# Cosformer attention into a GeGLU block: the third block of the feed-forward layer in groups with seven-product pairs, and the order of the blocks before it

## The chip, the cores and the metric

The kernel runs on one core of one Trainium2 chip. The metric is the device time of one execution, in microseconds. All times below are microseconds unless they are marked otherwise.

## The reference, cut to what matters

```python
# q, k, v: (8 batches, 8 heads, 576 positions, 64)
theta = np.pi / 2.0 * pos / S
phi(x) = concatenate([relu(x) * cos(theta), relu(x) * sin(theta)])   # 128 features
kv = einsum('bhsf,bhsd->bhfd', phi(k), v);  z = sum(phi(k), over s)
x  = (phi(q) @ kv) / (phi(q) @ z + 1e-6)         # as (4608 tokens, 512)
out = (gelu(x @ w_gate) * (x @ w_val)) @ w_out   # 512 -> 1536 -> 512
```

## The kernel before

**Tiling.** The 4608 tokens are nine blocks of 512 (block 0 to 8). A batch has 576 tokens, so that the batches lie across the blocks: block 3, tokens 1536 to 2047, takes the last 192 tokens of batch 2 and the first 320 of batch 3. Block n of the feed-forward layer is interleaved by hand with the attention of the next batch and with the output product of block n - 1. Nothing is scheduled by a planner: each engine, and the DMA queue of SP, executes what it was given in the order in which the program text issues it. A tile that has one buffer (`qT`, `vx`) is written again when the last reader of its old contents is done.

**Attention of a batch b.** The loads put q, k and v into staging buffers (`st`, which has three places, and for early batches `sm` and `fs`; `stage` says which). `prep` scales one ninth of q or k (128x256) with the cosine (VectorE, line 179) or the sine (ScalarE, line 177) into `phis`, which has three places, one for k; `prep_both` does q and k at once (128x512, lines 191 and 193). `cast_v` casts v into `vx`. `turn_q` turns the scaled q with two DMA transposes on SP into `qT`. `kv_unit` makes the 128x65 matrices of all heads with 72 small matmuls (line 270) in PSUM banks 6 and 7, and ScalarE copies them out. `nm_unit` makes the numerators and denominators of 128 tokens in two banks (6 and 7 if nothing else is said; line 311), and VectorE normalises them in three instructions (lines 322 to 324) into `x_sb`. `turn_x` turns that with DMA transposes on SP into `xT` of the block or blocks it belongs to (line 378); the first two batches are turned on TensorE instead (`turn_x_pe`, line 386, with a copy in line 390).

**A plain unit** (`gv_unit(n, jt)`, jt from 0 to 11) makes 128 of the 1536 hidden columns for 512 tokens: four matmuls of 512 columns against w_gate, a gelu on ScalarE (line 439), four against w_val (line 430), and the product on VectorE (line 442) into `hT`. Units take two pairs of banks in turn, (0, 1) and (2, 3). Where the tokens come late, the first units of a block are done in two halves of 256 tokens.

**A seven-product pair** (`Pair`) makes two hidden tiles for both matrices with seven products in place of eight, each four matmuls of 256 columns (line 650), from sums of the weights (S1 to S4 in `ws`, made by `w_sum`, line 616) and sums of the block's tokens (T1 to T4 in `fs`, made by `x_sum` on POOL, line 630). A **group** (`group`, line 700) is one pair and one plain unit with three slots of the other work between their products; four groups make a block. Blocks 4 and 5 are in groups, blocks 6 to 8 in pairs alone, blocks 0 to 3 in plain units.

**The output product** (`o_step`, `product`, line 547) is done from block 1 on in seven-product form too, 14 products of six matmuls of 256 columns for a block. The sums of hT that they need (`h_sum`, line 529) are made on VectorE for blocks 1 and 2 and on POOL from block 3 on. From block 3 on (`joint`) products 1 and 2 go into one bank one after the other, and one copy is saved.

**The order in blocks 1 to 3** stands in one loop (lines 985 to 1057) with tables: `COMING` and `q3` (what is scaled and cast in which step), `LOADS`, `SUMS`, and `t_kv`, `t_nm`, `t_turn` (the step of the kv matrices, of the first numerators and of the turn of q). In block 2 that is step 6 for kv of batch 3, steps 7 to 11 for its numerators, and the turn of its q comes after step 1. The last two tiles of batch 2 have their numerators in steps 0 and 1 of block 2.

Of the kernel before, what the change touches and what calls it, by code (L numbers as in the profile page):

```python
# [16 lines left out]
def kernel(  # L17
# [13 lines left out]
    nc = tc.nc  # L31
# [52 lines left out]
    def stage(name, b):  # L84
        early = {
            ("q", 1): 1, ("k", 1): sm, ("v", 1): fs, ("k", 2): 2, ("v", 2): 1,
            ("q", 3): fs, ("k", 3): 2, ("v", 3): 1,
            ("q", 5): 1, ("k", 5): 0, ("q", 7): 1, ("k", 7): 0,
        }
        at = early.get((name, b), "qkv".index(name))  # L90
        if isinstance(at, int):
            return st[:, at]
        return at[:, 0:NP * R * D].rearrange("p (m x) -> p m x", m=NP)
# [71 lines left out]
    def phi_tile(name, b):  # L165
        phi[name, b] = phis[:, 1 if name == "k" else 2 * (b % 2) * (b > 3)]
        return phi[name, b]
# [370 lines left out]
    def product(n, p, i, u, m, v):  # L538
# [5 lines left out]
        last = n == NB - 1  # L544
        joint = not last and n > 2
        for j in range(JH):
# [15 lines left out]
        if i in (6, 7) or i == (2 if joint else 1) or last and i == 5:  # L562
            k, of = (1, u) if i == 2 else (i, at)
            got[key, k] = place(n, p, f"u{k}", CH, FP32)
            (dve_copy if n in (3, 4) else act_copy)(got[key, k], of)  # L565
        if i == (2 if last or joint else 1):
# [268 lines left out]
    q1 = {9: (0, 1, 2), 10: (3, 4, 5), 11: (6, 7, 8)}  # L835
    early_sums = {5: ("S1", 0), 6: ("S1", 512), 7: ("S3", 0), 8: ("S3", 512)}
    for jt in range(4, JT):
        gv_unit(0, jt)
        if jt in early_sums:
            name, j0 = early_sums[jt]  # L840
            w_sum(name, j0, j0 + 512)
        if jt == 5:
            turn_j(0, 0, 4, (R - 1,), 4, act_copy)
        if jt == 6:
            nm_unit(0, 4)
        if jt == 8:
            turn_x_pe(0, 4, 5, act_copy)
        if jt in q1:
            prep("q", 1, 0, q1[jt])
            prep("q", 1, 1, q1[jt], eng=nc.scalar)  # L850
# [46 lines left out]
    def js(a, b):  # L897
        return tuple(range(a, b))

    COMING = {  # L900
        2: {
            3: [("k", 3, js(0, 3))], 4: [("k", 3, js(3, 6)), ("v", 3, 0)],
            5: [("k", 3, js(6, 9)), ("v", 3, 2)],
            7: [("q", 4, js(0, 3))], 8: [("q", 4, js(3, 6))], 9: [("q", 4, js(6, 9))],
            10: [("k", 4, js(0, 3))], 11: [("k", 4, js(3, 6))],
        },
        3: {
            0: [("k", 4, js(6, 9))], 1: [("v", 4, 0)], 2: [("v", 4, 2)],
            7: [("qk", 5, js(0, 2))], 8: [("v", 5, 0), ("qk", 5, js(2, 4))],
            9: [("v", 5, 2), ("qk", 5, js(4, 6))], 10: [("qk", 5, js(6, 8))],  # L910
            11: [("qk", 5, js(8, 9))],
        },
    }
    casts = {
        (3, 0): act_copy, (3, 2): act_copy, (4, 0): act_copy, (4, 2): dve_copy,
        (5, 0): nc.gpsimd.tensor_copy, (5, 2): nc.gpsimd.tensor_copy,
    }
    LOADS = {
        (1, 11): [(3, "k"), (3, "v")],
        (2, 1): [(4, "q", 0, 4), (4, "q", 4, R)], (2, 6): [(4, "k"), (4, "v")],  # L920
        (2, 10): [(5, "k")], (3, 0): [(5, "q")], (3, 2): [(5, "v")],
        (3, 10): [(6, "q", 0, 5), (6, "k", 0, 5)],
        (4, 0): [(6, "q", 5, R), (6, "k", 5, R), (6, "v")],
# [4 lines left out]
        2: {0: "1", 1: "2", 2: "34", 3: "56", 6: "78"},  # L928
        3: {0: "1", 1: "23", 2: "4", 3: "56", 4: "7", 6: "8"},
        8: {i: str(i + 1) for i in range(8)},  # L930
    }
    for n in range(4, 8):
        SUMS[n] = {0: "1", 1: "23", 2: "4", 3: "5", 4: "6", 5: "7", 6: "8"}


    MORE = {}
    for n in (4, 5, 6):
        for i in range(4):
            MORE.setdefault((n - 1, 8 + i), []).append((n, i))
# [6 lines left out]
    def more(n, jt):  # L946
# [6 lines left out]

    q3 = {
        (1, 8): ((0,), (0, 1)),
        (1, 9): ((1,), (2, 3)),
        (1, 10): ((2,), (4, 5)),
        (1, 11): ((3, 4, 5), (6, 7)),
        (2, 0): ((6, 7), (8,)),
        (2, 1): ((8,), ()),  # L960
    }

    def late_of(b):
        return -(-(BLK - 64 * b) // 128)

    def o_step(n, jt):
        p, u = divmod(jt, 6)
        for i in ((1, 2) if n > 3 else (2, 1), (5,), (6,), (7,), (4,), (3,))[u]:
            product(n - 1, p, i, ps[:, 4, 0:CH], ps[:, 5, 0:CH], ps[:, 4, CH:C])
        for i in map(int, SUMS[n].get(jt, "")):  # L970
            eng = nc.gpsimd if n > 3 else nc.vector
            h_sum(n - 1, i // 5, f"S{(i - 1) % 4 + 1}", eng=eng)
# [10 lines left out]

    turn[0] = 1
    for n in range(1, 4):
        b = n + 1

        t_kv, t_nm, t_turn = {1: (7, 9, 12), 2: (6, 7, 11), 3: (3, 5, 9)}[n]
        for jt in range(JT):
            if n == 1 and jt >= t_nm:  # L990
                nm_unit(2, jt - t_nm, (6, 4, 6)[jt - t_nm])
                turn_x(2, jt - t_nm)
            heads = (0, 2, 4, 4)[n]
            if jt >= heads:
                gv_unit(n, jt, to=(2, 6) if (n, jt) == (3, JT - 1) else None)
            else:
                for i in range(2):
                    half, unit = divmod(2 * jt + i, heads)
                    gv_unit(n, unit, half * HALF, HALF)
                    if n == 1:  # L1000
                        j = JA + 2 * jt + i
                        prep("q", b, 1, (j,), eng=nc.scalar)
                        prep("q", b, 0, (j,))
                        if jt == i == 0:
                            turn_x_pe(1, 3, 5, dve_copy)
            i = jt - t_nm - 1
            if n > 1 and 0 <= i < late_of(b):
                turn_x(b, i)
            if n > 1:
                o_step(n, jt)  # L1010
            elif jt % 3 == 1:
                flush()
            if n == 1 and jt == 2:
                prep("q", b, 0, (R - 1,))
                prep("q", b, 1, (R - 1,), eng=nc.scalar)
                turn_q(b)
                nm_unit(1, NT - 1)
            if n == 1 and jt == 3:
                turn_x(1, NT - 1)
            nms = [(b, jt - t_nm)] if n > 1 and 0 <= jt - t_nm < NT else []  # L1020
            if n == 2 and jt < 2:
                nms.append((n, 3 + jt))
            for bt in nms:
                nm_unit(*bt)
            if jt == t_kv:
                kv_unit(b)
            if n == 1 and jt in (2, 3, 4):
                prep_third("k", b, jt - 2)
            if n == 1 and jt == 5:
                cast_v(b, 0, 4, dve_copy)  # L1030
            if (n, jt) in q3:
                cosines, sines_ = q3[n, jt]
                prep("q", 3, 1, sines_, eng=nc.scalar)
                prep("q", 3, 0, cosines)
            for name, c, what in COMING.get(n, {}).get(jt, ()):
                if name == "v":
                    cast_v(c, what, what + 2, casts[c, what])
                elif name == "qk":
                    for j in what:
                        prep_both(c, 0, j, nc.scalar if j % 2 else nc.vector)  # L1040
                        prep_both(c, 1, j, nc.scalar)
                else:
                    prep(name, c, 0, what)
                    prep(name, c, 1, what, eng=nc.scalar)
            c = {(2, 1): 2}.get((n, jt), b if n > 1 and jt == t_turn else None)
            if c is not None and n < 3:
                turn_q(c + 1)
            start_loads(n, jt)
            c = {(2, 1): 2, (3, 2): 3, (3, 9): 4}.get((n, jt))
            if c is not None:  # L1050
                for i in range(late_of(c), NT):
                    turn_x(c, i)
            if n == 3 and 3 <= jt < 7:
                w_sum(("S2", "S2", "S4", "S4")[jt - 3], (1 - jt % 2) * 512, (2 - jt % 2) * 512)
            if n == 1 and 4 <= jt < 8:
                wo_sum(("T3", "T1", "T2", "T4")[jt - 4])
            more(n, jt)

# [6 lines left out]
    def preps(n, jt):  # L1067
        b = n + 1
        if 4 <= b < B - 1:
            for what in PREPS.get(jt, "").split():  # L1070
                prep_both(b + 1, "cs".index(what[0]), int(what[1]), nc.scalar)

    def numerators(n, jt):
        b, t = n + 1, {6: 0, 7: 1, 9: 2, 10: 3, 0: 4}.get(jt)
        if jt == 0:
            b = n
        if t is not None and b > 4:
            nm_unit(b, t)
# [27 lines left out]
    def slot(n, jt):  # L1106
        if (n, jt) != (4, 0):
            o_step(*divmod(n * JT + jt - 1, JT))
# [11 lines left out]
    old, made = None, 0  # L1120
    for n in range(4, NB):
        groups = {4: 4, 5: 4}.get(n, 0)
        for g in range(groups):
# [61 lines left out]
```

## Time and profile before

| | |
|---|---|
| three runs | 310.57, 310.44, 310.0 (median 310.44) |
| the profiled execution | 311.0 |
| its span, first to last instruction | 309.0 |
| granted TensorE clock | 1.0 |
| TensorE busy | 296.7 |
| VectorE, ScalarE, POOL busy | 234.4, 193.9, 137.6 |

PE is TensorE's matmuls, PEld its weight loads, DVE VectorE, ACT ScalarE, POOL GpSimd and SPq the DMA queue of SyncE. A line of the timeline or of the groups gives start and length, the engine, the line of the kernel, the operation and its tiles as out<-in; in square brackets stands the idle time of the engine before it and what ended it. A line of the waits gives who waited for whom, the sum, the number of times and the longest. In the chain, each line is a piece of the path that ended last: start, length, what.

### The profile page before, as it was taken

To read this page: it belongs to the slowest core of one execution; us is meant where nothing else is said; L and a number is where in the kernel's file an instruction comes from. 1 tells how busy PE (TensorE), PEld (TensorE's weight loads), DVE (VectorE), ACT (ScalarE), POOL (GpSimd) and SP (SyncE) were. 2 spreads that over 40 slices of the span, in tenths; PEclk is the share of its full clock that TensorE was granted. 3 is DMA by queue.
4 is the path that set the end of the run, shared out by engine and by line. 5 is a ranking of instruction groups with operands and counts; after the bars stand their busy time and mean duration, and the time that the engine had idled before them with its cause. 6 is when DMAs were issued, how large, how long until landed. Compare 5 with 4: busy or idle time off the path is not lost.

```text
span 309.0 us, 7855 instructions
## 1 busy us (share of the span) xinstructions
PE 296.7 (96%) x3032; PEld 223.6 (72%) x3055; DVE 234.4 (76%) x513; ACT 193.9 (63%) x393; POOL 137.6 (45%) x118
## 2 busy tenths in 40 slices
PE   8899999999999989999999999999999999999993
PEld 3574466645876668665778787878898988888882
DVE  5855896799896897789678967894678785766782
ACT  7864774866468756349597858785546456465530
POOL 6775440000000000017854686579965866297410
PEclk9999999999999999999999999999999999999999
DMA  7999999974698999993999799937732421203035
GB/s 273 257 185 245 313 308 398 302 116 70 187 230 155 281 325 229 280 195 78 261 118 352 177 176 140 357 69 114 120 76 53 80 44 36 54 16 68 2 80 127
DMA packets 71637, 53.66 MB, mean 174 GB/s; under 512 B 45392, under 2 KB 59472, under 8 KB 71600
## 3 DMA queue, kind: packets, MB, share of 16 engines
q1 hardware_dynamic: 61824, 41.17, 59.1%
q0 software_dynamic: 9696, 11.93, 16.8%
q8 instruction: 24, 0.39, 0.5%
q14 instruction: 13, 0.11, 0.2%
q10 hardware_dynamic: 80, 0.07, 0.1%
HBM read 37.75 MB, written 9.44 MB: 153 GB/s over the span
## 4 chain that ended last, share of the span: by engine, by line
PE 75%; DMA 9%; issue 5%; ACT 4%; DVE 3%; POOL 1%; SPq 1%; POOLq 0%; ACTq 0%; DVEq 0%
PE ps L650 24%; PE ps L430 23%; PE ps L547 18%; PE ps L463 3%; PE ps L311 3%; DMA st<-in_v_dram 3%; DMA qT<-phis 2%; DMA xT<-x_sb 2%; ACT phis L191 2%; PE ps L270 2%; DMA st<-in_k_dram 2%; ACT phis L177 1%; ACT gel L439 1%; PE ps L233 1%; PE ps L401 1%
## 5 line engine op out<-in xcount | busy, mean ns | idle before, releaser
L430 PE MATMUL ps<-xT,wv_sb 128*128 128x512 bf16 (+1 forms) x253 | 56.8, 345 | 0.4 <-ACT gel L439 0.3
L430 PE MATMUL ps<-xT,wg_sb 128*128 128x512 bf16 (+1 forms) x240 | 54.5, 344 | 2.8 <-DMA xT<-x_sb 1.2
L442 DVE TENSOR_TENSOR hT<-gel,ps 128x512 bf16<-128x512 f32 (+1 forms) x64 | 38.2, 602 | 15.5 <-PE ps L430 13.6
L439 ACT ACTIVATE gel<-ps 128x512 f32<-128x512 f32 (+1 forms) x64 | 33.7, 528 | 24.6 <-PE ps L430 22.3
L208 POOL CAST vx<-st 128x1152 bf16<-128x1152 f32 x6 | 7.1, 1179 | 91.8 <-DMA st<-in_v_dram 91.8
L430 PEld LDWEIGHTS <-wv_sb 128*128 128x128 bf16 x256 | 25.0, 98 | 20.5 <-issue 0.4
L529 POOL TENSOR_TENSOR sm<-hT 128x768 bf16<-128x768 bf16 x20 | 32.8, 1638 | 15.8 <-PE ps L650 11.5
L547 PEld LDWEIGHTS <-sm 128*128 128x128 bf16 x336 | 32.9, 98 | 6.8
L430 PEld LDWEIGHTS <-wg_sb 128*128 128x128 bf16 x256 | 23.3, 98 | 16.7 <-DMA xT<-x_sb 1.4
L650 PE MATMUL ps<-fs,ws 128*128 128x256 bf16 x240 | 34.5, 273 | 0.2 <-ACT ps L669 0.2
L650 PEld LDWEIGHTS <-ws 128*128 128x128 bf16 x320 | 30.2, 98 | 4.1 <-ACT ps L669 0.5
L682 ACT ACTIVATE gel<-ps 128x512 f32<-128x512 f32 x26 | 15.5, 597 | 28.0 <-PE ps L650 28.0
L177 ACT ACTIVATE phis<-st,sin_t 128x256 bf16<-128x256 f32 (+1 forms) x75 | 31.5, 484 | 2.2 <-DMA st<-in_k_dram 1.3
L560 DVE TENSOR_TENSOR o_sb<-sm,ps 128x256 f32<-128x256 f32 x56 | 23.5, 419 | 12.1 <-ACT sm L565 11.0
L547 PEld LDWEIGHTS <-hT 128*128 128x128 bf16 x288 | 28.2, 98 | 5.4
L690 DVE TENSOR_TENSOR ps<-fs,ps 128x512 f32<-128x512 f32 x26 | 18.1, 696 | 18.0 <-PE ps L650 13.7
L650 PE MATMUL ps<-xT,wg_sb 128*128 128x256 bf16 x208 | 31.2, 273 | 0.0
L324 DVE TENSOR_TENSOR x_sb<-ps,rec 128x512 bf16<-128x512 f32 x38 | 26.3, 692 | 1.3
L547 PE MATMUL ps<-wo_sb,hT 128*128 128x256 bf16 x192 | 23.7, 273 | 0.0
L547 PE MATMUL ps<-T,sm 128*128 128x256 bf16 x168 | 22.9, 273 | 0.1
L650 PEld LDWEIGHTS <-wg_sb 128*128 128x128 bf16 x208 | 20.1, 98 | 4.0
L547 PE MATMUL ps<-wo_sb,sm 128*128 128x256 bf16 x168 | 22.9, 273 | 0.0
(126 smaller groups left out, 563.1 us busy)
## 6 DMA issues: line engine op xcount, KB each, us to landing
out_dram<-o_sb SPq DMA_DIRECT2D x69, 128.0 KB, 2.5
st<-in_v_dram SPq DMA_DIRECT2D x12, 576.0 KB, 6.9
st<-in_k_dram SPq DMA_DIRECT2D x8, 576.0 KB, 5.1
st<-in_q_dram SPq DMA_DIRECT2D x4, 640.0 KB, 5.9
st<-in_q_dram POOLq DMA_DIRECT2D x4, 576.0 KB, 12.4
st<-in_q_dram SPq DMA_DIRECT2D x4, 512.0 KB, 5.1
wg_sb<-in_moe_w_gate_dram POOLq DMA_DIRECT2D x6, 256.0 KB, 6.4
wv_sb<-in_moe_w_val_dram POOLq DMA_DIRECT2D x6, 256.0 KB, 7.3
```

Of the source, the lines that this page charges most:

```text
L177: nc.scalar.activation(o, i, AF.Relu, scale=tab[:, j:j + 1])
L311: nc.tensor.matmul(bank(b0 + h // 4)[:, (h % 4) * (D + 1):(h % 4 + 1) * (D + 1)], lhsT=q_cols(b, t, h), rhs=kv_sb[b][:, h // 2, h % 2, :], ...
L324: nc.vector.tensor_tensor(x, nm[:, :, :, 0:D], rec[:, :, :, None].to_broadcast([128, 2, 4, D]), op=ALU.mult,)
L430: nc.tensor.matmul(bank(to[g])[:, 0:w], lhsT=wt[:, ct, js], rhs=xt[:, ct, c0:c0 + w], start=(ct == 0), stop=(ct == CT - 1),)
L439: nc.scalar.activation(gel[:, 0:w], bank(to[0])[:, 0:w], AF.Gelu)
L442: nc.vector.tensor_mul(hT[n][:, jt, c0:c0 + w], gel[:, 0:w], bank(to[1])[:, 0:w])
L529: eng.tensor_tensor(a[name][:, j0:j1], a[x][:, j0:j1], a[y][:, j0:j1], op=op)
L547: nc.tensor.matmul(at, lhsT=hs.setdefault(key, h_parts(n, p))[a][:, j], rhs=ts[b][:, j], start=(j == 0 and i in ((1, 2, 4, 5), (1, 4, 5))[ ...
L560: nc.vector.tensor_tensor(o, got[key, k], x, op=op)
L650: nc.tensor.matmul(to[:, 256 * half:256 * half + 256], lhsT=w_part(a, j * 128, (j + 1) * 128)[:, ct], rhs=xb[self.n][b][:, ct], start=(hal ...
L682: nc.scalar.activation(self.gel0, self.other, AF.Gelu)
L690: nc.vector.tensor_tensor(bank(val), self.m5, self.sum, op=ALU.add)
```

## The change

Block 3 joins blocks 4 and 5 in groups, so that its tokens' sums, its hidden sums' place on POOL and the joint products 1 and 2 begin one block earlier. All eight halves of the weights' sums are made in block 0. The loop over blocks 1 to 3 becomes one function for block 1 and one for block 2:

- Batch 2: v is cast on ScalarE in steps 3 and 4 of block 1 (before: on VectorE in step 5); the kv matrices come in step 6 (before: 7); the first numerators come inside unit 9, between its two matmul groups (before: ahead of it). The turn of batch 1's fourth tile goes between the two matmul groups of block 1's first unit.
- Batch 3: k is loaded in step 2 and v in step 5 of block 1 (before: both at the end of its step 11), k into `sm`; q is scaled in steps 5 to 9 of block 1 into a place of its own, k in steps 10 and 11; q is turned after step 11. In block 2 v is cast in step 0, the kv matrices come in step 1, the numerators in steps 5 to 9, and each turn of x one step after its numerators, ahead of the loads of that step.
- Batch 4: q and k are loaded from step 10 of block 1 on and scaled together in steps 2 to 10 of block 2, v is cast on POOL. Batch 5 is loaded from step 9 of block 2 on and scaled in block 3, as batch 6 is in block 4.

```diff
@@ def stage
-            ("q", 3): fs, ("k", 3): 2, ("v", 3): 1,
+            ("q", 3): fs, ("k", 3): sm, ("v", 3): 2,
@@ def phi_tile
-        phi[name, b] = phis[:, 1 if name == "k" else 2 * (b % 2) * (b > 3)]
+        phi[name, b] = phis[:, 1 if name == "k" else 2 * (b % 2) * (b > 2)]
@@ def product
-        joint = not last and n > 2
+        joint = not last and n > 1
-            (dve_copy if n in (3, 4) else act_copy)(got[key, k], of)
+            (dve_copy if n in (2, 3, 4) else act_copy)(got[key, k], of)
@@ block 0
-    early_sums = {5: ("S1", 0), 6: ("S1", 512), 7: ("S3", 0), 8: ("S3", 512)}
+    early_sums = {4: ("S1", "S3"), 5: ("S2", "S4"), 6: ("S1",), 7: ("S3", "S2"), 8: ("S4",)}
@@ LOADS
-        (1, 11): [(3, "k"), (3, "v")],
-        (2, 1): [(4, "q", 0, 4), (4, "q", 4, R)], (2, 6): [(4, "k"), (4, "v")],
-        (2, 10): [(5, "k")], (3, 0): [(5, "q")], (3, 2): [(5, "v")],
-        (3, 10): [(6, "q", 0, 5), (6, "k", 0, 5)],
+        (1, 2): [(3, "k")], (1, 5): [(3, "v")],
+        (1, 10): [(4, "q", 0, 5), (4, "k", 0, 5)], (1, 11): [(4, "q", 5, R), (4, "k", 5, R)],
+        (2, 1): [(4, "v")],
+        (2, 9): [(5, "q", 0, 5), (5, "k", 0, 5)],
+        (3, 0): [(5, "q", 5, R), (5, "k", 5, R), (5, "v")],
+        (3, 9): [(6, "q", 0, 5), (6, "k", 0, 5)],
@@ def o_step
-            eng = nc.gpsimd if n > 3 else nc.vector
+            eng = nc.gpsimd if n > 2 else nc.vector
@@ the loop over blocks 1 to 3, now two functions
+    def scale(b, name, sines_, cosines):
+        for j in sines_:
+            prep(name, b, 1, (j,), eng=nc.scalar)
+        for j in cosines:
+            prep(name, b, 0, (j,))
+
+    SCALE = {
+        2: (2, "k", js(0, 3), js(0, 3)), 3: (2, "k", js(3, 6), js(3, 6)),
+        4: (2, "k", js(6, 9), js(6, 9)),
+        5: (3, "q", js(0, 1), ()), 6: (3, "q", js(1, 3), js(0, 1)),
+        7: (3, "q", js(3, 5), js(1, 3)), 8: (3, "q", js(5, 7), js(3, 6)),
+        9: (3, "q", js(7, 9), js(6, 9)),
+        10: (3, "k", js(0, 4), js(0, 4)), 11: (3, "k", js(4, 9), js(4, 9)),
+    }
+
+    def block1():
+        b, n = 2, 1
+        for jt in range(JT):
+            i = jt - 9
+            if i > 0:
+                nm_unit(b, i, (6, 4, 6)[i])
+                turn_x(b, i)
...
+                    x3 = lambda: turn_x_pe(1, 3, 5, dve_copy)
+                    gv_unit(n, unit, half * HALF, HALF, between=x3 if jt == i == 0 else None)
...
+                gv_unit(n, jt, between=(lambda: nm_unit(b, 0, 6)) if i == 0 else None)
...
+            if jt == 6:
                 kv_unit(b)
+            if jt in SCALE:
+                c, name, sines_, cosines = SCALE[jt]
+                scale(c, name, sines_, cosines)
+            if jt in (3, 4):
+                cast_v(b, 2 * (jt - 3), 2 * (jt - 3) + 2, act_copy)
+            if jt == 11:
+                turn_q(3)
             start_loads(n, jt)
...
+    EARLY = {
+        2: "s0", 3: "c0 s1 c1", 4: "s2 c2", 5: "s3 c3", 6: "s4 c4", 7: "s5 c5", 8: "s6 c6",
+        9: "s7 c7", 10: "s8 c8",
+    }
+
+    def block2():
+        b, n = 3, 2
+        for jt in range(JT):
...
+            if 0 <= jt - 6 < NT:
+                turn_x(b, jt - 6)
+            o_step(n, jt)
+            if 0 <= jt - 5 < NT:
+                nm_unit(b, jt - 5)
+            if jt < 2:
+                nm_unit(2, 3 + jt)
+            if jt == 0:
+                cast_v(b, 0, 2, dve_copy)
+                cast_v(b, 2, 4, act_copy)
+            if jt == 1:
+                kv_unit(b)
+            for what in EARLY.get(jt, "").split():
+                part = "cs".index(what[0])
+                prep_both(4, part, int(what[1]), nc.scalar if part or jt > 7 else nc.vector)
+            if jt == 1:
+                turn_x(2, 3)
+                turn_x(2, 4)
+            start_loads(n, jt)
+            if jt in (7, 8):
+                m = 2 * (jt - 7)
+                cast_v(4, m, m + 2, nc.gpsimd.tensor_copy)
             more(n, jt)
@@ the blocks in groups
-    for n in range(4, NB):
-        groups = {4: 4, 5: 4}.get(n, 0)
+    for n in range(3, NB):
+        groups = 4 if n < 6 else 0
```

`SUMS`, `MORE` (the sums of the tokens), `preps`, `numerators` and `slot` take block 3 in where they began with block 4.

## The prediction

> **What bounds the kernel now.** I read the page first, for busy shares.
>
> ```profile
> span 309.0 us, 7855 instructions
> PE 296.7 (96%) x3032; PEld 223.6 (72%) x3055; DVE 234.4 (76%) x513; ACT 193.9 (63%) x393; POOL 137.6 (45%) x118
> ```
>
> TensorE is the bound, at a granted clock of 1.0 throughout, so time is won by giving it fewer columns or fewer waits. Then busy time by stretch, cut where the blocks 1 to 5 begin on TensorE:
>
> ```profile
> core 0: us, PE busy (x) PEld busy (x) DVE busy (x) ACT busy (x) POOL busy (x), PEclk, DMA share, GB/s
> 54.20:78.40 24.20, 23.39 (x221) 13.27 (x222) 21.63 (x54) 16.95 (x40) 0.00 (x0) 1.00 0.70 155
> 78.40:113.30 34.90, 33.45 (x340) 23.80 (x340) 29.29 (x82) 23.21 (x54) 0.00 (x0) 1.00 1.00 241
> 113.30:146.60 33.30, 32.71 (x321) 23.07 (x325) 27.86 (x61) 19.61 (x41) 7.11 (x6) 1.00 0.90 201
> 146.60:178.10 31.50, 30.80 (x332) 24.36 (x334) 24.83 (x48) 23.57 (x41) 19.89 (x14) 1.00 0.96 227
> 178.10:209.30 31.20, 30.99 (x340) 24.95 (x343) 24.30 (x50) 23.15 (x41) 21.72 (x15) 1.00 0.91 181
> ```
>
> The first figure is the length, the next TensorE's busy time. Blocks 4 and 5 are already grouped and take 31.5 and 31.2; block 3 has the same attention and output products and takes 33.3. In block 1 VectorE is busy 21.63 of 24.20: the fullest engine after TensorE, and the change gives it more there. TensorE's waits between 54 and 160 us, and the chain around two of them:
>
> ```profile
> PE ps L430 <- DMA xT<-x_sb: 1.2, 1, 1.2
> PE ps L430 <- DVE xT L390: 0.5, 1, 0.5
> ```
>
> ```profile
> 65.47 7.25 DMA qT<-phis
> ...
> 106.39 6.91 DMA xT<-x_sb
> 113.35 1.92 PE ps L430 x16
> ```
>
> The transpose of 106.39 lands after 6.91 us, where the issue itself is 1.2: four loads were issued from 101.86 to 104.68 and it lands behind them. TensorE stood from 111.92 to 113.35. Last, the timeline, for the two things that I expect to decide:
>
> ```profile
> 101.14 0.42 PE L311 MATMUL ps<-kv_sb,qT 128*128 128x65 bf16 x8
> ...
> 102.03 0.69 DVE L324 TENSOR_TENSOR x_sb<-ps,rec 128x512 bf16<-128x512 f32 x1
> ...
> 102.64 0.87 DVE L179 TENSOR_SCALAR phis<-st,cos_t 128x256 bf16<-128x256 f32 x3
> ```
>
> ```profile
> 133.05 0.42 PE L311 MATMUL ps<-kv_sb,qT 128*128 128x65 bf16 x8
> ...
> 135.35 0.69 DVE L324 TENSOR_TENSOR x_sb<-ps,rec 128x512 bf16<-128x512 f32 x1
> ...
> 136.10 0.42 PE L311 MATMUL ps<-kv_sb,qT 128*128 128x65 bf16 x8 [0.25 <-DVE x_sb L324]
> ```
>
> From the first: VectorE normalises the numerators of banks 6 and 7 by 102.72, 1.25 after TensorE is through with them (101.47), and a 0.69 instruction holds VectorE for 0.61 before the next starts. From the second: whoever writes banks 6 and 7 next waits until that has ended (136.04, then 136.10).
>
> **What the change wins.** Block 3 in groups: each of four pairs runs 28 matmuls of 256 columns for what was 32, at 0.109 each (eight start in 0.87), 4 x 4 x 0.109 = 1.74 of TensorE. Its products, numerators, scalings, value casts and x sums become those of block 4 one batch earlier, so I take block 4's length for it: 33.3 to 31.5, 1.8. The sums for the products go from VectorE (0.55 each) to POOL (1.64) as in block 4, where POOL is busy 19.89 of 31.5. Block 4 is then no longer the first in groups and takes block 5's length, 0.3. The wait at 113.35 goes, 1.4 with its issue gap: numerators of batch 3 come at steps 5 to 9 of block 2 instead of 7 to 11, and their transposes stand on SP behind no load issued in those steps before step 9. I put the last that block 3 needs at about 110, the block at about 115, which leaves POOL 4 x 1.15 for the x sums. At the start of block 1 the turn of the last x moves between the two matmul groups of the first unit; the second half starts at 56.3 instead of 56.98, 0.7. The wait for qT at 72.45 (0.3 lost) goes, since the numerators come half a unit later. In all 4.5.
>
> **What it costs.** W sums: four more in block 0, at 0.61 of VectorE each. Adding the queue up from unit 4 (eight sums, five products of 0.60, one numerator set of 1.04), VectorE is up to 0.4 late and free again at 35.3, before the product due at 35.68. So 0; if that cover is gone, the turn of q waits for its cosines at 39, up to 0.4. Nothing there leaves TensorE's path, so it cannot gain.
>
> Value casts of batch 2 go from VectorE (1.36) to ScalarE (2 x 1.15, in units 3 and 4). ScalarE falls 2.4 behind by the gelu of unit 5; the bank it frees is wanted only after kv of batch 2, which now stands between units 6 and 7 with 1.27 of work. So 0; without that cover 0.7.
>
> Scaling of k of batch 3 moves into units 10 and 11 of block 1, behind which VectorE still has the numerators' normalising and products. Its queue from the product of unit 2 (at 59.9 with the 0.7 won) to the normalised x of batch 2's last tile in block 2: ten products x 0.60, 28 cosines x 0.26, four sets of numerators x 1.04, four sums of w_out x 0.87, together 21.0; then four half products x 0.33, two sets x 1.04, a cast 0.67, two sums x 0.46, one addition 0.33, together 5.3; and 1.5 in which it waits for ScalarE's late gelus and one copy. That ends at 87.7. The same sum for the old order ends the product of unit 11 at 79.8, against 79.66 in the trace, so I take 87.5.
>
> Two waits follow. At the start of block 2 the second unit reuses the bank pair of unit 11, whose product ends at about 80.8; and x of batch 2 lands behind the loads of k and v of batch 3, now issued in block 1 after qT (landed at 72.0 then, four loads at 1.5 each, 78.7). TensorE, which came 1.0 early, finishes unit two 0.5 later than before: cost 1.5, between 0 (no backlog) and 2.5 (first load 2.7 behind qT, as at 98.57 to 101.22 now).
>
> The second: kv of batch 3 moves from step 6 of block 2 to step 1, directly behind the numerators of batch 2's last tile, both in banks 6 and 7. Queued behind that wait on TensorE is everything. TensorE arrives at 85.2 (84.64 now plus 0.5), VectorE frees the banks at 87.5: 2.3. The floor with an idle VectorE is 1.25, from the row above. It can't be zero, since the banks are the same. The Trainium skill's page "PSUM — Partial Sum Buffer", in its summary of rules for kernel authors, wants a matmul to go to another bank than the one being read; no run yet shows this change with other banks, but by that rule kept the sum would be 2.3 lower.
>
> On SP, turning q of batch 3 waits for those same numerators (qT has one buffer), and the second halves of q and k of batch 4, two turns of x and v of batch 4 queue behind it. It landed 10.9 after issue at 61.84 and 13.0 in block 4; numerators of batch 3 come 13.2 after (kv 1.4, four steps of 2.4, the hold). I take 0, up to 0.5.
>
> **The sum.** 311.0 profiled (309.0 and 2.0 around the span) - 4.5 + 1.5 + 2.3 = 310.3. The profiled run lies 0.56 over the median of 310.44, so on the median 309.7.
>
> **Rivals.** (A) VectorE keeps up: for it, each engine's row sums are averages with 2.6 idle in block 1; against it, the work added there. Then nothing at block 2's start and 1.25 for the banks: -3.2, 307.2. (B) VectorE's queue is longer than added up: den, rec and x start with gaps of 0.03 between them; if all 68 instructions of the queue paid that, 2.0 more before kv, so +1.3, 311.7: slower. It decides from 88.8 on for the normalised x (the forecast has 87.5). For it, that the whole stretch is one queue with no slack; against it, that rows of 0.69 do start 0.60 apart. (C) The loads in block 1 land x of batch 2 at 80.1: block 2 begins 1.4 later, but VectorE catches up meanwhile, the hold shrinks to 1.3 or so, net about -0.3, 310.1. (D) The loads of batch 4 hold x of batch 3 after all, and the wait before block 3 stays: 1.4 more, 311.1; the transposes' place argues against it.
>
> **How the numbers follow.** Forecast 0.36 (own range 308.9 to 310.5), A 0.22, B 0.22, C 0.12, D 0.08. What the measurement can tell from no change is 0.2%, 0.62: below 309.82 faster, above 311.06 slower. Faster: A and 0.25 of the forecast, 0.47. Slower: B, D in part, together 0.30. The rest, 0.23, is C, D and the forecast's upper end. The range of 308.0 to 311.8 leaves out the far end of A and of B.
>
> **What would show it.** Right: block 3 about 31.5 long; no wait on xT before it; in block 2 a wait of kv (L270) on x_sb (L324) of 1.3 to 2.5; VectorE without idle from about 68 to 87. Wrong: no such wait (A), or one over 3.5 (B), or a wait on xT before block 2 of over 2 (C) or before block 3 (D), or a grouped block 3 longer than 32.

## The result, and the profile after

| | before | after |
|---|---|---|
| median of four runs each, on the same chip | 310.5 (310.0 to 311.74) | 320.66 (318.71 to 321.46) |
| ratio | | 1.0312, interval 1.0256 to 1.0368 |
| profiled execution, its span | 311.0, 309.0 | 321.46, 319.7 |
| mean granted clock in it | 1.000 | 0.977 |

The change makes the kernel slower by 3.1%. The forecast was 309.7, with a range of 308.0 to 311.8. Executions over 1.5% above the shortest of their kernel (two in run 1 below, one in 6, three in 9, one in 11) are left out of the ratios, while the medians are of all. From the page of the kernel after, busy time of TensorE and its granted clock in 40 slices:

```profile
PE   7799999999579979999999999999999999999992
PEclk9799999999789979999999999999999999999999
```

The losses lie in slices 11 to 15, 80 to 120 us. The row of the clock, all nines before, has four dents: one in the start (slice 2) and one in each of the slices 11, 12 and 15, where PE has its dents. Busy time by stretch, cut where the first matmuls of block 0, 1, 3, 4 and 5 stand, and for block 2 where its first could have stood (length first, then TensorE):

```profile
core 0: us, PE busy (x) PEld busy (x) DVE busy (x) ACT busy (x) POOL busy (x), PEclk, DMA share, GB/s
18.15:56.20 38.05, 37.50 (x375) 22.35 (x377) 28.60 (x68) 23.17 (x49) 15.40 (x22) 1.00 1.21 295
56.20:79.60 23.40, 23.24 (x221) 13.28 (x221) 21.21 (x56) 20.83 (x48) 0.00 (x0) 1.00 0.98 225
79.60:125.53 45.93, 37.73 (x337) 26.06 (x340) 30.69 (x73) 21.25 (x44) 6.84 (x6) 0.89 0.77 172
125.53:156.50 30.97, 30.53 (x329) 24.25 (x331) 22.88 (x47) 22.97 (x40) 19.72 (x14) 1.00 0.85 200
156.50:187.47 30.97, 30.76 (x338) 24.72 (x341) 24.08 (x50) 23.06 (x40) 19.83 (x14) 1.00 0.94 207
```

Against the same stretches of before (38.02, 24.20, 34.90, 33.30, 31.50): block 0 has the same length, block 1 is 0.8 shorter, block 3 2.3 and block 4 0.5, and block 2 grew from 34.9 to 45.9. That is 7.4 more. Nearly all of the rest of the 10.7 between the spans is at the two ends: block 0 starts 2.0 later (18.15 against 16.18), and from the last matmul to the end it takes 6.2 against 5.05. The late start is not the change's: over the profiles of this study it is 16.2 to 18.2 whatever the kernel, and 18.08 in one that differs from the kernel before only in block 1 and later. It goes with the dent in slice 2: in the six profiles in which the clock falls at about 11 us block 0 begins at 17.0 to 18.2, in the ten others at 16.2 to 17.1. TensorE's waits:

```profile
PE ps L430 <- DMA xT<-x_sb: 3.5, 1, 3.5
PE ps L270 <- DVE x_sb L324: 2.3, 1, 2.3
PE ps L311 <- DVE x_sb L324: 2.2, 1, 2.2
```

So there are three holes in block 2 (stretches in which TensorE waits), and a clock that drops after each.

**The first hole: x of batch 2 is late.** SyncE's queue, and the piece of the chain that ends the wait:

```profile
71.72 1.87 SPq L98 DMA_DIRECT2D sm<-in_k_dram  x2
73.68 1.17 SPq L378 DMA_TRANSPOSE xT<-x_sb  x1
75.03 0.96 SPq L98 DMA_DIRECT2D st<-in_v_dram  x2
76.93 3.61 SPq L378 DMA_TRANSPOSE xT<-x_sb  x2
```

```profile
76.93 6.29 DMA xT<-x_sb
83.21 0.14 issue
83.35 3.35 PE ps L430 x16
```

The transpose of 76.93 is issued in time and lands 6.29 later, behind k, x of batch 1 and v. In the kernel before the transposes of this stretch landed 2.4 to 3.1 after their issue. TensorE stood from 79.8 to 83.35.

**The second hole: kv of batch 3 waits for the banks.** The chain just ahead of it:

```profile
90.30 0.75 DVE vx L208
91.05 0.66 DVE hT L442 x2
91.71 0.47 DVE sm L529
92.29 0.21 DVE rec L323
92.52 0.70 DVE x_sb L324
93.27 2.16 PE ps L270 x72
```

A cast, two half products and a sum stand on VectorE ahead of the normalising that frees banks 6 and 7. VectorE brings no lateness there from block 1: behind the first hole it has nothing to do for 1.40.

```profile
85.32 0.42 DVE L442 TENSOR_TENSOR hT<-gel,ps 128x256 bf16<-128x256 f32 x1 [1.40 <-PE ps L430]
```

**The third hole, which the forecast did not have.** The timeline before the numerators of step 7:

```profile
109.69 1.14 POOL L208 CAST vx<-st 128x1152 bf16<-128x1152 f32 x1 [64.30 <-DMA st<-in_v_dram]
109.75 1.48 DVE L529 TENSOR_TENSOR sm<-hT 128x768 bf16<-128x768 bf16 x1
111.12 1.15 POOL L208 CAST vx<-st 128x1152 bf16<-128x1152 f32 x1 [0.29 <-PE ps L430]
111.17 1.51 DVE L529 TENSOR_TENSOR sm<-hT,sm 128x768 bf16<-128x768 bf16 x1
113.77 0.60 PE L311 MATMUL ps<-kv_sb,qT 128*128 128x65 bf16 x8 [2.15 <-DVE x_sb L324]
```

Two of VectorE's sums, 0.55 each elsewhere, take 1.48 and 1.51. Each begins 0.05 to 0.06 behind a cast of v of batch 4 on GpSimd and ends 0.40 to 0.41 behind that cast's end. The Trainium skill's page "SBUF — State Buffer", section "SBUF: two separate sides", says that GpSimd and a VectorE instruction with two SBUF inputs take a shared pair of ports as an exclusive lock for a whole instruction. The rows nearly agree: a sum that waits for the whole cast would end 0.55 behind it, and these ended 0.40 and 0.41 behind.

**The clock.** Stretches of 3.41 us, cut at the instants at which the granted clock changes; PEclk, the granted clock, is the third figure from the end:

```profile
79.50:82.92 3.42, 0.30 (x2) 0.00 (x0) 3.35 (x11) 2.79 (x7) 0.00 (x0) 1.00 1.34 226
82.92:86.34 3.42, 2.99 (x15) 2.10 (x16) 1.42 (x5) 0.62 (x2) 0.00 (x0) 0.50 1.09 348
86.34:89.75 3.41, 3.41 (x39) 3.08 (x38) 1.65 (x6) 1.85 (x5) 0.00 (x0) 1.00 0.30 82
89.75:93.17 3.42, 1.18 (x17) 1.06 (x15) 3.35 (x8) 0.28 (x2) 0.00 (x0) 1.00 0.28 42
93.17:96.58 3.41, 3.31 (x78) 2.89 (x78) 0.04 (x1) 0.74 (x3) 0.00 (x0) 0.50 0.90 130
110.23:113.64 3.41, 1.38 (x10) 0.80 (x9) 3.34 (x6) 1.11 (x2) 1.75 (x2) 1.00 0.26 17
113.64:117.06 3.42, 3.29 (x15) 1.42 (x15) 2.43 (x7) 0.60 (x1) 0.00 (x0) 0.50 0.44 90
```

All changes lie on one grid of 3.41. A stretch in which TensorE was busy 0.30, 1.18 or 1.38 is followed by one at half clock, that is at a granted clock of 0.50. So each hole costs its length and then up to half of 3.41 again.

### The profile page after: what moved, and what is told of

It reads as the page before. It is cut to its first block, busy times and chain, and to the rows that moved or that the text cites. A ratio compares the mean times of both kernels' runs of the same rounds, so it can differ in the third digit from the quotient of the medians.

```text
span 319.7 us, 7881 instructions
## 1 busy us (share of the span) xinstructions
PE 299.6 (94%) x3047; PEld 228.4 (71%) x3071; DVE 231.8 (73%) x497; ACT 198.9 (62%) x390; POOL 155.6 (49%) x132
## 3 DMA queue, kind: packets, MB, share of 16 engines
q0 software_dynamic: 9696, 11.93, 16.2%
## 4 chain that ended last, share of the span: by engine, by line
PE 80%; DVE 5%; issue 5%; DMA 4%; ACT 2%; POOL 1%; SPq 0%; POOLq 0%; DVEq 0%; ACTq 0%
PE ps L650 28%; PE ps L430 20%; PE ps L547 19%; PE ps L463 3%; PE ps L311 3%; PE ps L270 3%; DMA st<-in_v_dram 2%; DMA xT<-x_sb 2%; PE ps L233 1%; DVE sm L529 1%; ACT phis L177 1%; DVE hT L442 1%; PE ps L401 1%; DVE x_sb L324 1%; PE ps L386 1%
## 5 line engine op out<-in xcount | busy, mean ns | idle before, releaser
L430 PE MATMUL ps<-xT,wg_sb 128*128 128x512 bf16 (+1 forms) x190 | 47.4, 366 | 4.5 <-DMA xT<-x_sb 3.5
L529 POOL TENSOR_TENSOR sm<-hT 128x768 bf16<-128x768 bf16 x24 | 39.4, 1643 | 20.8 <-DVE hT L442 9.8
L430 PE MATMUL ps<-xT,wv_sb 128*128 128x512 bf16 (+1 forms) x206 | 49.5, 363 | 0.1
L442 DVE TENSOR_TENSOR hT<-gel,ps 128x512 bf16<-128x512 f32 (+1 forms) x52 | 32.4, 624 | 20.2 <-PE ps L430 17.4
L650 PE MATMUL ps<-fs,ws 128*128 128x256 bf16 x288 | 41.7, 273 | 0.2 <-ACT ps L669 0.2
L439 ACT ACTIVATE gel<-ps 128x512 f32<-128x512 f32 (+1 forms) x52 | 28.3, 548 | 21.0 <-PE ps L430 19.6
L650 PEld LDWEIGHTS <-ws 128*128 128x128 bf16 x384 | 36.2, 98 | 4.9 <-ACT ps L669 0.5
L650 PE MATMUL ps<-xT,wg_sb 128*128 128x256 bf16 x240 | 36.0, 273 | 0.0
L529 POOL TENSOR_TENSOR sm<-hT,sm 128x768 bf16<-128x768 bf16 x12 | 19.7, 1643 | 15.5 <-PE ps L547 13.1
L191 ACT ACTIVATE phis<-st,sin_t 128x512 bf16<-128x512 f32 x36 | 25.8, 716 | 0.0
```

The source lines that it names most:

```text
L191: nc.scalar.activation(o, i, AF.Relu, scale=tab[:, j:j + 1])
L430: nc.tensor.matmul(bank(to[g])[:, 0:w], lhsT=wt[:, ct, js], rhs=xt[:, ct, c0:c0 + w], start=(ct == 0), stop=(ct == CT - 1),)
L439: nc.scalar.activation(gel[:, 0:w], bank(to[0])[:, 0:w], AF.Gelu)
L442: nc.vector.tensor_mul(hT[n][:, jt, c0:c0 + w], gel[:, 0:w], bank(to[1])[:, 0:w])
L529: eng.tensor_tensor(a[name][:, j0:j1], a[x][:, j0:j1], a[y][:, j0:j1], op=op)
L650: nc.tensor.matmul(to[:, 256 * half:256 * half + 256], lhsT=w_part(a, j * 128, (j + 1) * 128)[:, ct], rhs=xb[self.n][b][:, ct], start=(hal ...
```

## The experiments

A program was timed in alternation with the kernel before, whose median was 310.8 to 311.3 in all of them. The "body" below is worked out from each profile: from the first product of block 0 to the end of the last matmul. It leaves out both ends: 287.8 before (16.24 to 303.99), 295.3 after. It is that of one execution for each kernel, and the profiled one can lie at the edge: it is the longest of four for the kernel after, the second longest of ten in run 1 and the shortest of four in run 3.

**1. The load of v of batch 3 alone, later.**

```diff
-        (1, 2): [(3, "k")], (1, 5): [(3, "v")],
+        (1, 2): [(3, "k")], (1, 9): [(3, "v")],
```

> The loads of v of batch 3 go from step 5 to step 9 of block 1, behind the turn of batch 2's first x. Theory (each wait of TensorE over about 2 us costs its length and 1.7 more, since the granted clock is 0.5 for 3.41 us after it): the wait on xT before block 2 (3.5) shrinks to under 1, the half clock at 83 us goes, 4 to 5 us less than the changed kernel, 315.5 to 317. Rival (VectorE's queue holds the stretch, and a wait removed comes back at the next place): the wait of kv for x_sb grows from 2.3 to over 3.5 and less than 2 us is won.

Measured: 314.11, ratio 1.0072 (1.0032 to 1.0111). One load alone is moved, the wait on xT before block 2 is gone, and the body is 290.8, 4.5 shorter than after. The hold on kv stays at 2.3 and brings the half clock. The executions in the ratio differ with the mean clock: 311.05 in one at 0.998, 315.5 in one at 0.986.

**2. The kv unit of batch 3 one step later.**

```diff
-            if jt == 1:
+            if jt == 2:
                 kv_unit(b)
```

> The kv matrices of batch 3 go from step 1 to step 2 of block 2, behind a unit and an output product. Theory: the hold of 2.3 for banks 6 and 7 and the half clock at 93 us go, 3.5 to 4 us less, 316.5 to 317.5. Rival (VectorE's queue): the wait stays over 1 us at the later place, under 2 us won.

Measured: 314.93, ratio 1.0128 (1.0084 to 1.0172).

```profile
PE ps L430 <- DMA xT<-x_sb: 4.6, 1, 4.6
PE ps L311 <- DVE x_sb L324: 0.3, 1, 0.3
```

The hold on kv is gone. So is most of the third: without the second hole the sums run at 106.1 to 107.1, ahead of the casts on GpSimd (from 109.6 on), and take 0.55 again. So the third hole needs both: the casts on GpSimd, and the delay that brings the sums beside them. The wait on xT stays. Body 289.3.

**3. Dummy products in the three holes.** 15 before block 2, 9 before kv of batch 3 and 9 before the numerators of step 7, 512 columns each, into a bank that the next unit takes.

```diff
+            if jt == 0:
+                warm(15)
...
+            if jt == 7:
+                warm(9)
...
             if jt == 1:
+                warm(9)
                 kv_unit(b)
```

> Matmuls of 512 columns on data that nobody uses fill most of the three waits of block 2: 15 ahead of block 2, 9 ahead of kv of batch 3, 9 ahead of the numerators of step 7. Nothing else moves, so that the real work waits as long as before. Theory of the clock: the granted clock stays 1.0 through block 2 and up to 3 x 1.7 = 5.1 us are won, 315 to 316.5. Rival (the clock falls for another reason, or costs nothing since VectorE and the transfers set the pace there): the half clock stays, or goes with less than 2 us won.

Measured: 316.29, ratio 1.0156 (1.0111 to 1.0201). No half clock is left in the body:

```profile
PEclk9999999999999999999999999999999999999999
```

The body is 290.7 against 295.3: three half clocks were worth 4.6, 1.5 each. The medians (320.66 and 316.29) differ by 4.4. The holes themselves are still there, filled with dummies.

**4. All three causes undone:** the edits of 1 and 2, and the casts of v of batch 4 on ScalarE.

```diff
-                cast_v(4, m, m + 2, nc.gpsimd.tensor_copy)
+                cast_v(4, m, m + 2, act_copy)
```

> v of batch 3 loaded in step 9 of block 1, kv of batch 3 in step 2 of block 2, and v of batch 4 cast on ScalarE in place of POOL. Theory: no wait of TensorE over 1.5 us and no half clock in blocks 1 to 3; what is left is the gain of the change, 4 to 5 us less than the kernel before: 305.5 to 307. Rival (VectorE's queue): waits of 2 us or more stay, 309 to 313.

Measured: 312.44, ratio 1.0063 (1.0031 to 1.0095), body 288.1. The time is in the rival's range, but both waits that are left begin with a transfer, not with VectorE:

```profile
PE ps L430 <- DMA xT<-x_sb: 2.9, 1, 2.9
PE ps L430 <- ACT phis L177: 1.4, 1, 1.4
```

v now stands ahead of the second and third tile of batch 2's x, and the wait on xT comes in the second half of block 2's tokens. The other wait is ScalarE's: its gelu stands behind the scaling of k of batch 3, which begins at 77.9 when its load lands.

**5 and 6. The loads put in another order, with and without the other two edits.**

```diff
     for m in (0, 2):
         load(nc.sync, "q", 3, m, m + 2)      # end of block 0
+    for m in (0, 2):
+        load(nc.sync, "k", 3, m, m + 2)
-        (1, 2): [(3, "k")], (1, 5): [(3, "v")],
+        (1, 5): [(3, "v")],
-        (1, 10): [(4, "q", 0, 5), (4, "k", 0, 5)], (1, 11): [(4, "q", 5, R), (4, "k", 5, R)],
+        (1, 11): [(4, "q", 0, 5), (4, "k", 0, 5)],   # the second halves behind turn_q(3)
-        2: "s0", 3: "c0 s1 c1", ...                  # scaling of batch 4
+        3: "s0", 4: "c0 s1 c1", ...
```

> Keys and values of batch 3 by batch 4's unit: kv unit of batch 3 one step later, v of batch 4 cast on ScalarE, and the loads put where nothing of block 2 waits behind them: k of batch 3 at the end of block 0 beside its q, v of batch 3 at step 5 as in the changed kernel, q and k of batch 4 behind the last transposed x of batch 2, their scaling one step later. If it is the order of the load queue that makes block 2 wait, there is no wait on xT over 0.5, none on x_sb over 0.5 and no half clock in the body; from the first product of block 0 to the first of block 4 it takes 126.6 (the kernel with all three undone took 131.2, of which 4.6 were waits), and the time is 306 to 308. If the queue is full whatever the order (the rival), a wait of 2 to 4 is found at another place of blocks 1 or 2, and the time is 310 to 313.

Measured, with all: 310.76, ratio 0.9979 (0.9949 to 1.001), no difference from before that can be told, in the rival's range. The profiled execution, 313.73, is the longest of its ten: body 288.4, a wait of 2.3 on xT, a half clock at 83.2 and

```profile
76.54 5.56 DMA xT<-x_sb
```

The queue between: v lands at 81.60, this transpose at 82.10. k and the loads of batch 4 are out of its way, v is not.

> The changed kernel with the loads alone put as in the kernel that undoes all (k of batch 3 at the end of block 0, q and k of batch 4 behind the last x of batch 2 and scaled a step later); kv unit and casts stay. Load theory: the wait of 3.5 on xT before block 2 goes, and the half clock after it: 3.7 + 1.6 less, about 315.3, the hold on kv stays at 2.3 or grows to 3, since VectorE has no wait in which to catch up. Rival (transposes of the turned q, not the loads, set when x lands): wait of 3 or more remains, 319 to 321.

Measured, loads alone (with the scaling of batch 4 a step later): 312.5, ratio 1.004 (1.0011 to 1.0069), body 289.8. The order of the loads takes back most of what the change lost, though 1.5 of the wait on xT is left; the third hole is 1.2 in place of 2.2, since only one of the two sums stands beside a cast here (1.50, the other 0.55).

```profile
PE ps L270 <- DVE x_sb L324: 2.3, 1, 2.3
PE ps L430 <- DMA xT<-x_sb: 1.5, 1, 1.5
PE ps L311 <- DVE x_sb L324: 1.2, 1, 1.2
```

The hold on kv is 2.3 in kernels whose wait on xT was 3.5 (after), 1.5 (this one) and none (run 1): it does not shrink when VectorE has had time to catch up, nor grow when it hasn't.

**7. The casts of v of batch 4 on ScalarE, alone** (the edit shown under 4, on the kernel after).

> The changed kernel with only the two casts of v of batch 4 moved from GpSimd to ScalarE. If the casts on GpSimd slow VectorE's two sums from 0.55 to 1.5 each, the sums take 0.55 again, the wait of the numerators of step 7 falls from 2.2 to under 0.5 and the half clock after it goes: 2 + 1.6 less, about 317. If the sums are slow for another reason (their operands, the banks), they stay at 1.5 and the time at 320.5.

Measured: 318.3, ratio 1.0233 (1.0173 to 1.0294). The sums beside no cast:

```profile
112.34 0.55 DVE L529 TENSOR_TENSOR sm<-hT 128x768 bf16<-128x768 bf16 x1
112.81 0.55 DVE L529 TENSOR_TENSOR sm<-hT,sm 128x768 bf16<-128x768 bf16 x1
```

and the wait of the numerators of step 7 is 0.3. So the casts made the sums slow, and the third hole with them. In this profile the wait on xT was 4.9 (3.5 in that of after) with two stretches at half clock behind it in place of one, so that its body of 294.5 shows less than the hole was worth.

**8. The kernel before with the loads of batch 3 sooner.** One line of the old program:

```diff
-        (1, 11): [(3, "k"), (3, "v")],
+        (1, 5): [(3, "k"), (3, "v")],
```

> The kernel before with one edit: k and v of batch 3 are loaded at step 5 of block 1 instead of step 11, into the same places. Load theory: their four halves, which land 1.4 apart, stand ahead of the transposed x of batch 2 and block 2 waits 3 to 4 on xT; with a half clock behind it (1.6) where the wait fills a stretch of the clock's grid: 313 to 316. Rival (the order of the loads is harmless and the wait comes from VectorE, which in this kernel has less to do there): 309.5 to 310.8.

Measured: 315.08, ratio 1.0142 (1.0079 to 1.0206), body 290.1.

```profile
76.77 7.86 DMA xT<-x_sb
84.76 1.25 PE ps L430 x10
```

With nothing else of the change, loading sooner makes the wait before block 2: TensorE waits 3.8 for it, until 84.76, and the body is 2.3 longer (the wait before block 3 became shorter; the rest of the 4 is a late start, 18.08, in that execution, and the starts of the others are not known). The clock stayed at 1.00, though the hole is longer than that of after. It lies across a border of the grid:

```profile
79.35:82.76 3.41, 1.56 (x7) 0.53 (x6) 3.13 (x9) 1.58 (x4) 0.00 (x0) 1.00 1.39 357
82.76:86.17 3.41, 1.41 (x13) 1.30 (x14) 0.26 (x1) 0.38 (x1) 0.00 (x0) 1.00 1.02 95
86.17:89.59 3.42, 3.42 (x39) 3.09 (x37) 1.71 (x6) 1.46 (x5) 0.00 (x0) 1.00 0.00 0
```

**9. The load of v of batch 3 on GpSimd's queue** (on the kernel of 5; cast a step later).

```diff
+            if jt == 5:
+                for m in (0, 2):
+                    load(nc.gpsimd, "v", 3, m, m + 2)
```

> The last kernel with the loads put in order, the kv unit a step later and the casts on ScalarE still waited 2.3 on xT before block 2: x of batch 2 landed 0.5 behind the second half of v of batch 3 (81.60 and 82.10). Here that load alone goes to GpSimd's queue at the same step 5, and is cast a step later. If it is the order within SyncE's queue that holds x, x lands within 4 of its issue, the wait before block 2 and the half clock behind it go, and the time is 306 to 308 (2.5 of wait and 1.6 of half clock less than 310.8). If the transfers share what carries them (the rival: it is the bytes under way, 78% of the DMA engines' time there, whatever queue they stand in), x of batch 2 still lands after 81 and the time is 309.5 to 311.

Measured: 314.88, ratio 1.0078 (1.0035 to 1.0121).

```profile
67.21 11.11 DMA qT<-phis
```

The time is outside both, the cause is the rival's: the load, issued at 66.7 from the other queue, ran beside the turn of q of batch 2, whose second half now took 11.11 instead of 6.34 (67.95 to 74.29 after), and TensorE waited 5.4 on qT. The other queue did not help: the load began sooner there, and its bytes slowed a transpose of SyncE's queue. "DMA: Bandwidth & Descriptors" of the Trainium skill says so under "Issuing engines are not separate DMA queues": DMAs issued by different engines run on the same 16 DMA engines. The 78% of the expectation is not what run 5 shows: its DMA share from 72.0 to 82.1 is 1.02.

**10 and 11. The load of v of batch 3 behind the last x of batch 2** (on the kernel of 5).

```diff
-        (1, 5): [(3, "v")],
-        (1, 11): [(4, "q", 0, 5), (4, "k", 0, 5)],
+        (1, 11): [(3, "v"), (4, "q", 0, 5), (4, "k", 0, 5)],
-        (2, 1): [(4, "v")],
+        (2, 3): [(4, "v")],                  # in 11 only
```

> The same kernel with the load of v of batch 3 on SyncE's queue again, but behind the last transposed x of batch 2 (step 11, ahead of q and k of batch 4), its casts and the kv unit of batch 3 two and one steps later. Both theories take the bytes out of the way of x of batch 2: no wait on xT before block 2, 306 to 308. What would be late instead is the cast: v lands near 87, the kv unit stands at about 90, so up to 1 of wait on vx there; q and k of batch 4 land near 90, two steps before ScalarE scales them. If block 2 waits elsewhere as much as it waited on xT, the time is 309.5 to 311.

In run 10 v of batch 4 was loaded into the same place ahead of the casts of step 2, so batch 3 was computed with v of batch 4, and its casts waited for that load: 16.3 of wait on vx, 327.65, ratio 1.0527 (1.049 to 1.0563). It tells only that the wait on xT is gone.

> The kernel with v of batch 3 loaded behind the last transposed x of batch 2 once more, and v of batch 4, which goes into the same place, two steps later than there (step 3 of block 2, behind the casts of v of batch 3). With v of batch 3 out of the way x of batch 2 landed at 79.42 in the last run, and there was no wait on xT. Load theory: from the first product of block 0 to the first of block 4 it takes 126.6 to 128, no half clock in the body, 306.5 to 308.5. Rival (block 2 waits elsewhere as much): up to 2 of wait on vx or on gel behind q and k of batch 4, which land at 91 to 94, and 309.5 to 311.

Measured: 311.45, ratio 1.0018 (0.9986 to 1.005), just above the rival's range. The body is 286.3, 1.5 shorter than before, without a wait on xT or a half clock in it. What is late instead:

```profile
PE ps L311 <- DMA qT<-phis: 1.7, 2, 1.3
...
PE ps L430 <- DVE hT L442: 0.9, 1, 0.9
```

qT of batch 3 lands at 99.36, behind v, q and k.

**12. The W sums alone, in the kernel before** (the change's `early_sums`, without the sums in block 3).

> The kernel before with one part of the change: S2 and S4 of the W sums in steps 5, 7 and 8 of block 0 instead of steps 3 to 6 of block 3. Forecast for this part: 0. If VectorE's time in block 0 is on the path after all, four sums more there cost up to 2.5 (four of 0.6); if block 3 gains by what leaves it, up to 1 less.

Measured: 311.17, ratio 0.9999 (0.9974 to 1.0024): the forecast's 0.

**13. Dummy products before block 2 in the kernel of 5.**

```diff
+            if jt == 0:
+                dummies(12, 0 if turn[0] % 2 == 0 else 2)
```

> The kernel with loads in order, the kv unit a step later and the casts on ScalarE (310.8) with twelve dummy products of 512 columns (12 x 0.22) on TensorE ahead of block 2, where it waited 2.3 on xT. If the half clock behind that wait is still part of its time, it goes: 1.5 less, 309.3, while the wait itself stays. If the clock was not lowered in most of its executions, or the wait is shorter than the dummies, nothing is won: 310.8 to 311.3.

Measured: 312.54, ratio 1.0048 (1.0031 to 1.0065), a loss where a gain was looked for. All its executions had a mean clock of 0.995 or more, but so had seven of the ten of the kernel of 5: there was little to win. And with the hole filled the numerators of batch 3 come before their qT, which landed at 100.23; TensorE waited 1.1 for it.

**14. The kernel of 11 with k of batch 3 scaled later on VectorE.**

```diff
-        10: (3, "k", js(0, 4), js(0, 4)), 11: (3, "k", js(4, 9), js(4, 9)),
+        10: (3, "k", js(0, 4), ()), 11: (3, "k", js(4, 9), js(0, 4)),
+            if jt == 0:                          # block 2, behind its first two half units
+                scale(b, "k", (), js(4, 9))
```

> The kernel with v of batch 3 behind the last x of batch 2 (311.45), whose second unit of block 2 waited 0.9 on the product of unit 11 (hT, line 442), with the cosines of k of batch 3 later: four in step 11 and five in step 0 of block 2, where they were four in step 10 and five in step 11. If that wait is VectorE's backlog of units 10 and 11, as the forecast's first cost has it, it goes, and 0.9 of time: 310.5. If it has another cause, the wait and 311.45 stay.

Measured: 311.25, ratio 1.0005 (0.9987 to 1.0023). The wait on hT is gone and the body is 285.6, 2.2 shorter than before; the waits left are

```profile
PE ps L311 <- DMA qT<-phis: 1.7, 2, 1.2
```

The profiled execution, 309.51, was the shortest of its twelve, so the body of 285.6 need not be typical, and no gain is shown. None of the fourteen is shown to be faster than the kernel before. All kernels made from the change also take 5.3 to 6.2 from the last matmul to the end, where before and its two variants (8, 12) take 5.0. That eats up to 1 of it; its cause was not found.

## Why the prediction was wrong

Three things failed, all in block 2: the term for its start (1.5; a wait of 3.5 was measured), the casts on GpSimd, which stand in no term (2.2), and the clock, which stands in no term either (three times 1.5). The gains of blocks 1, 3 and 4 were right, 3.6 in place of 3.1.

**The start of block 2, forecast at 1.5 (0 to 2.5): the first step that failed.** The forecast put four loads behind qT, 1.5 each, at 78.7, and x of batch 2 with the last of them. It set qT well: landed 74.29 in an execution that began 2.0 later, so 72.3 against 72.0. But the last tile of batch 1 stands in that queue too, between k and v: unlike the batch's other tiles it is turned by a DMA transpose, in step 3 of block 1. It took 1.9 there; the first load landed 2.3 behind qT, not 1.5; and x lands behind them. x came at 83.2, 81.2 in the forecast's time, and the wait was 3.5, with a half clock of about 1.5 behind it. Rival C (chance 0.12) named this mechanism and its sign on xT (a wait of over 2), but priced x at 80.1 and let the wait be given back, at 310.1. Runs 1, 6 and 8 show the loads' place from both sides: moving one load (1) or all of them (6) in the changed kernel returns most of the loss, the sooner loads in the old one make the wait and a body 2.3 longer.

The rows that the forecast read did not give it away. In block 2 before, where these loads stood, the DMA share was 1.00 at 241 GB/s; from 71.96 to 78.40 of block 1, where they went, it was 0.22, so that there was room. What they took there was a place ahead of x. The old program issued k and v of batch 3 at the end of block 1, behind the x that block 2 needs first. The forecast took the sooner loads as a gain for block 3 and did not rank all that crosses the queue between 60 and 100 us by when it is needed. Runs 4, 5, 9 and 11 each moved a transfer and left another late: x of the second half (2.9), x of the first (2.3), qT of batch 2 (5.4), qT of batch 3 (1.7).

**VectorE's backlog there** was the reason given for 1.5. It is real, but covered in the changed kernel by the late x: with x in time (run 11) unit 2 waited 0.9 for the product of unit 11, and with nine cosines moved (run 14) it didn't.

**The hold on kv, 2.3:** measured 2.3, and that is luck. With the start 2.0 later the forecast has TensorE there at 87.2 and the banks free at 89.5; they came at 90.9 and 93.2. And the reason is another than the forecast's. VectorE had caught up during the wait on xT (the 1.40 above); what it has to do in the step itself (0.75 of cast, two products, a sum, the normalising) makes the 2.3, so it does not depend on how late VectorE was. For the same reason the hold did not shrink to 1.3 as rival C had it. One step of delay undid it (run 2). No run put kv into other banks. The floor of 1.25 is a misreading: by its row TensorE is through at 101.56 (101.14 and 0.42), which makes 1.16; of the prices only rival A's rests on it.

**The casts of v of batch 4 on POOL, in no term of the forecast:** 2.2. It speaks of the value casts of block 3, which become those of block 4; these are in block 2. In block 4 the hidden sums are on POOL too; in block 2 they are still on VectorE, beside the casts. Run 7 shows it. The sign was in the kernel before, in the same microseconds of block 3 from which the forecast took its third view:

```profile
133.45 1.14 POOL L208 CAST vx<-st 128x1152 bf16<-128x1152 f32 x1 [88.50 <-DMA st<-in_v_dram]
133.99 1.01 DVE L529 TENSOR_TENSOR sm<-hT,sm 128x768 bf16<-128x768 bf16 x1
```

A sum of 0.55 takes 1.01 there and ends 0.41 behind the cast, as in the third hole.

**The clock, in no term of the forecast:** three times 1.5 (run 3). A wait's price went into the sum at its own length, so that even the 2.3 that was forecast for kv was 1.5 too small. This is the largest part of what block 2 lost beyond the forecast.

**What held.** W sums at 0 (run 12). Block 3: 33.3 to 30.97, 2.3 against 1.8 forecast. Block 4: 0.5 against 0.3. Block 1: 0.8, against 0.7 and 0.3. No wait on xT before block 3.

So of a miss of 11.2 in the profiled execution (321.46 against 310.3), block 2 holds 8.6: it grew by 11.0 instead of 2.4 (1.5 and 2.3, less 1.4). The measured parts make nearly that: waits of 3.5, 2.3 and 2.2 and three half clocks of 1.5, less the 1.4, are 11.1. Of the rest 2.0 is the start, 1.1 the end; the blocks around it gave 0.5 more than forecast.

## What to carry to other kernels

Before loads are moved ahead, write down everything that crosses the same queue in that stretch in the order of issue, transposes included, and set beside each when its reader needs it: a transfer that is "sooner" is in front of another. Price a wait on TensorE with what follows it, a half clock that can add 1.5 to a hole of 2.2. And when an instruction goes to GpSimd, look at what VectorE runs in the same microsecond.

## What the runs showed of the hardware

- In blocks 1 to 3 the granted clock fell to 0.5 for a stretch of 3.41 after a stretch of the same grid in which TensorE was busy 1.38 or less (the kernel after) or 1.40 (run 10), and didn't after 1.41 and 1.56 (run 8). Busy time alone does not set the bound: before block 0 it fell after 1.57, 1.60 and 1.90 too (runs 11, 5 and 2). The Trainium skill's "TensorE: Matmul & The Clock Gate" describes a free-running window of 3413 ns (Part 1) and, in "HAM oscillation — how this bites in real kernels", gives as the rule no idle gaps over about 3.4. Here waits of 2.2 and 2.3 inside one stretch were enough, and one of 3.8 across two was not; the measurement decides.
- VectorE's 128x768 sums of two bf16 operands took 1.48 and 1.51 beside a cast on GpSimd (1.01 where the cast had begun 0.54 sooner), 0.55 alone.
- One program's time went with its mean clock: run 1 gave 311.05 at 0.998 and 315.5 at 0.986. That the place of its holes on the grid decides this is argued from the rows of run 8, not shown.
